# The first batch's plain-head results go straight into the mixing tiles, its token operands get buffers ahead of the last weights, and the tables load later

## The chip, the core and the metric

The kernel runs on one core of one Trainium2 chip. The metric is device time in microseconds (us) of that core, from the first to the last instruction and what lies around them. The engines are named as the profile names them: PE is TensorE (matmuls) and PEld its weight loads, DVE is VectorE, ACT is ScalarE, POOL is GpSimd, SP is SyncE, whose queue issues most DMAs. Each engine takes its instructions strictly in the order in which the program holds them.

## The reference

Eight batches of 576 tokens; eight heads of 64 columns, the first four with a plain window mask, the last four with a dilated one; then a mixing by Fourier transform over tokens and channels; then a normalised two-layer network with a residual.

```python
mask_plain = (rel >= 0) & (rel < 32)
mask_dil = (rel >= 0) & (rel < 128) & (rel % 4 == 0)
attn = softmax(where(mask[h], q @ k.T / 8, -1e9));  x = concat_heads(attn @ v)   # (8, 576, 512)
X = np.fft.fft(np.fft.fft(x, axis=1), axis=2)
u = x + np.real(X)
un = (u - mean(u)) / np.sqrt(var(u) + 1e-06)
out = u + np.maximum(un @ w_ch1, 0.0) @ w_ch2        # 512 -> 2048 -> 512
```

## The kernel before

All operations are put into one list (`Plan`), each with an engine, a planned cost and a priority; a planner written in the kernel goes through a model of time and emits the instructions in the order that it finds. The order on each engine is therefore fixed when the program is built. The numbers at the head of the file (`P_ST0`, `P_FD`, `P_MIX0`, `P_W` and so on) are due times, in units of one attention step, that set these priorities; `NSC2` and `NAV2` say for how many steps attention has two more PSUM banks.

**Attention** (`attention`, `attend_pair`, `attend`) makes 96 steps, 12 for each batch: two kinds of heads, two pairs of heads in each, three steps in each pair. A step is four score products on PE (L562), four masked row maxima on DVE (L571), four exponentials on ACT (L577), four transposes on PE (L590), a copy on ACT (L593), four products with the values on PE (L597), and three small operations on DVE (L605, L608, L609) that write the result tile `xt`. `store` (L644) sends `xt` to the DRAM tensors `xsp` and `xsm`, in which the token halves lie for the Fourier step.

**Mixing** (`mix`, one call for each batch) reads them back into four SBUF tiles `xs` and two tails `xtail` (L716, L725). `fold` adds and subtracts mirrored halves (L728, L730, L750, L752 on POOL, L742, L744 on DVE, L746, L747 on ACT); then come transforms along the tokens (L779, with tables `seq` and `tail`) and along the channels (L825, with tables `chn` and `alt`), the sums `u` (L693, L695 on POOL) and `normalise`. For the first batch `turned` transposes the normalised tokens on PE (L678) and splits them into a high and a low part (L685 on ACT, L686 on DVE) in a token tile `ut`; for the others the rows go through DRAM.

**Early network work** (`fill`): six of the 16 hidden blocks are computed for all 36 groups of 128 tokens, two in a call, while attention still runs: `up` (L959) needs a token tile `ut` and weights, `down` (L975) the hidden tile and weights. The rest of the network (L1228, L1283, L1316) follows once attention and mixing are done.

**Weights**: the twelve tiles for `fill` arrive as 64-bit floats. `prep_w` has each narrowed to 32 bits by four DVE operations (L900, L903, L906, L909) and one on ACT (L898), and split into a high part (L915 on ACT) and a low part (L917 on POOL). The staging tile of a weight and the token tile `ut` come from one ring of four buffers (`utb`), handed out in the order in which the program asks for them: the twelve weights first, then the two token tiles of the first batch. Buffer 13 of that sequence can be taken when the 9th weight has been read for the last time, by its L917.

**Filler**: L508 multiplies zeros. Wherever the planner has no other work for PE before the first `up`, it puts pairs of these products; from the first `up` on it puts none.

## Time and profile before

| what | value |
|---|---|
| median of 3 runs | 1077.82 us (1077.35 to 1078.23) |
| the profiled execution | 1077.06 us |
| its span, first to last instruction | 1075.3 us |
| PE busy, share of the span | 1062.8 us, 99% |
| filler among it (L508) | 240 products, 42.5 us, 1.4 to 116.4 us |
| DVE busy | 770.8 us, 72% |
| first `up` of the early network work | at 118.08 us |

The groups of instructions say where an engine's time goes, the windows say it by stage, and the timeline gives the order in time with the idle time in square brackets. Two records that follow each other on an engine can overlap, so that the sum of groups is larger than the engine's busy time, and PE counts as busy while it multiplies zeros.

### The profile page before, as it was taken

Reading aid. Unit: us, or ns where it says so; the run is one execution under the profiler, and the core shown is the slowest. Engines: PE = TensorE matmul, PEld = TensorE weight load, DVE = VectorE, ACT = ScalarE, POOL = GpSimd, SP = SyncE. Lnnn points to the kernel's source line nnn. Section 1 sums busy time; section 2 is a strip of 40 time slices with the busy share of each in tenths; the row PEclk is TensorE's granted clock in tenths of the full one; section 3 lists DMA queues with packets and bytes.
Section 4 is the critical chain, followed back from the end, with each engine's and each line's share of the span. In section 5 each row is a group of like instructions: output and inputs, shape, how many; then the busy total and the mean of one; then the engine's idle time right before and its main releaser. Section 6 shows DMA issues by size and latency. Waiting matters only on the chain.

```text
span 1075.3 us, 21155 instructions
## 1 busy us (share of the span) xinstructions
PE 1062.8 (99%) x7675; PEld 957.3 (89%) x7675; DVE 770.8 (72%) x2384; ACT 515.5 (48%) x1282; POOL 278.0 (26%) x328
## 2 busy tenths in 40 slices
PE   8999999999999999999999999999999999999998
PEld 7898988888888989998989898989999988989987
DVE  5989988878866765866675667677676767675845
ACT  6876755566464533444343443525252525252522
POOL 1247364554633355132321110101010101010200
PEclk9999999999999999999999999999999999999999
DMA  9987464746644341634363302322323232232211
GB/s 345 301 253 229 147 194 138 215 142 188 191 134 144 98 128 41 194 121 126 129 158 96 101 26 54 108 71 96 73 91 84 86 87 82 69 100 81 79 60 40
DMA packets 103801, 137.10 MB, mean 128 GB/s; under 512 B 9145, under 2 KB 61817, under 8 KB 103697
## 3 DMA queue, kind: packets, MB, share of 16 engines
q1 hardware_dynamic: 100128, 126.85, 39.4%
q0 software_dynamic: 3040, 8.09, 2.5%
q8 instruction: 60, 0.98, 0.4%
q10 hardware_dynamic: 528, 0.82, 0.2%
q14 instruction: 45, 0.36, 0.1%
HBM read 97.92 MB, written 37.80 MB: 126 GB/s over the span
## 4 chain that ended last, share of the span: by engine, by line
PE 93%; DVE 2%; DMA 2%; ACT 1%; issue 0%; POOL 0%; POOLq 0%; ACTq 0%; DVEq 0%
PE bank L1228 23%; PE bank L1316 20%; PE bank L959 14%; PE bank L975 13%; PE bank L597 5%; PE bank L562 5%; PE bank L825 3%; PE bank L779 3%; PE bank L590 3%; PE bank L508 3%; PE bank L1283 1%; DMA vt<-in_v_dram 1%; DVE pm L571 1%; DMA ut<-in_w_dram 1%; ACT pm L577 1%; PE bank L801 1%
## 5 line engine op out<-in xcount | busy, mean ns | idle before, releaser
L1228 PE MATMUL bank<-low,wb 128*128 128x512 f32 x1080 | 260.4, 393 | 0.0
L1228 PEld LDWEIGHTS bank<-low,wb 128*128 128x128 f32 x1080 | 198.5, 188 | 40.8
L959 PE MATMUL bank<-ut,low 128*128 128x256 f32 x1296 | 170.8, 285 | 0.1
L959 PEld LDWEIGHTS bank<-ut,low 128*128 128x128 f32 x1296 | 160.4, 189 | 3.2 <-DVE low L967 0.5
L975 PE MATMUL bank<-low 128*128 128x512 f32 x648 | 154.3, 392 | 0.0
L577 ACT ACTIVATE pm<-pm,mx 96x128 f32<-96x128 f32 x384 | 130.7, 395 | 39.5 <-DVE mx L571 37.7
L1003 POOL DMA_INDIRECT ut<-us,flip_sb x20 | 40.6, 2028 | 406.6 <-DVE ut L1060 249.8
L975 PEld LDWEIGHTS bank<-low 128*128 128x128 f32 x648 | 119.3, 188 | 23.1
L1234 ACT ACTIVATE xa<-bank 128x256 f32<-128x256 f32 x90 | 34.3, 382 | 179.9 <-PE bank L1228 179.9
L571 DVE CUSTOM_DVE_ANT_0 pm<-bank,mask_sb 96x128 f32<-96x128 f32 x384 | 93.3, 278 | 30.3 <-PE bank L562 27.6
L1255 DVE TENSOR_TENSOR y<-xa 128x384 f32<-128x384 f32 x45 | 25.1, 557 | 106.5 <-ACT xa L1234 106.2
L967 DVE SCALAR_TENSOR_TENSOR low<-bank,low 128x256 fp32r<-128x256 f32 x108 | 45.5, 422 | 62.0 <-ACT low L965 61.4
L597 PE MATMUL bank<-vt,ptsb 128*96 128x65 f32 x768 | 80.7, 247 | 2.5 <-DVE xt L609 1.5
L597 PEld LDWEIGHTS bank<-vt,ptsb 128*96 128x96 f32 x768 | 75.8, 164 | 6.9 <-ACT ptsb L593 1.6
L965 ACT ACTIVATE low<-bank 128x256 fp32r<-128x256 f32 x108 | 41.4, 384 | 79.4 <-PE bank L959 78.9
L1316 PEld LDWEIGHTS bank<-w2s,low 128*128 128x128 f32 x588 | 73.8, 190 | 2.4
L1049 DVE TENSOR_TENSOR ut<-ut,bank 128x512 f32<-128x512 f32 (+1 forms) x136 | 73.2, 547 | 2.6 <-PE bank L1228 0.5
L1082 DVE STREAM_TRANSPOSE ut<-ut 128x512 f32<-128x512 f32 (+1 forms) x76 | 71.6, 982 | 4.4 <-DMA ut<-us 4.2
L1316 PE MATMUL bank<-w2s,low 128*128 128x256 f32 x588 | 74.4, 282 | 0.0
L562 PE MATMUL bank<-kb,tq 64*96 64x128 f32 x768 | 63.0, 286 | 3.2 <-DVE mx L571 1.5
L593 ACT COPY ptsb<-bank 128x384 f32<-128x384 f32 x96 | 45.3, 472 | 35.8 <-PE bank L590 28.2
L1316 PEld LDWEIGHTS bank<-w2s,hm 128*128 128x128 f32 x483 | 59.8, 189 | 1.9
(147 smaller groups left out, 1817.3 us busy)
## 6 DMA issues: line engine op xcount, KB each, us to landing
vt<-in_v_dram SPq DMA_DIRECT2D x32, 390.0 KB
us<-uc SPq DMA_DIRECT2D x36, 257.0 KB
tq<-in_q_dram SPq DMA_DIRECT2D x32, 288.0 KB
part<-row SPq DMA_DIRECT2D x36, 256.0 KB
wst<-in_w_dram SPq DMA_DIRECT2D x18, 512.0 KB
ut<-us SPq DMA_DIRECT2D x36, 256.0 KB
ut<-part SPq DMA_DIRECT2D x36, 256.0 KB
kb<-in_k_dram SPq DMA_DIRECT2D x31, 288.0 KB
```

Of the source, the lines that this page charges most:

```text
L562: nc.tensor.matmul(sc()[e][:QB, KB * n:KB * n + KB], lhsT=tq()[ps, QB * t:QB * t + QB], rhs=kb()[ps, QB * t:QB * t + KB], start=True, stop ...
L571: nc.vector.tensor_tensor_reduce(pm()[:, i], sc()[i % 2][:QB, KB * (i // 2):KB * (i // 2) + KB], mask_sb()[:, masks[blocks[i // 2]]], -0.1 ...
L577: add("ACT", 0.295, lambda i=i: nc.scalar.activation(out=pm()[:, i], in_=pm()[:, i], func=AF.Exp, bias=mx()[:, i:i + 1], scale=-1.0), ((mx ...
L593: add("ACT", act(4 * QB) - 0.05, lambda: nc.scalar.copy(out=pt().rearrange("p i q -> p (i q)"), in_=ps()[:, :4 * QB]), (ps,), (pt,), prio)
L597: add("PE", 0.173, lambda i=i: nc.tensor.matmul(av()[:QB, 65 * i:65 * i + 65], lhsT=pt()[:, i], rhs=vt()[:, i % 2, blocks[i // 2]], start= ...
L959: nc.tensor.matmul(z()[:, :n_tok], lhsT=wf()[:, a, kk], rhs=ut()[:, p, kk], start=(kk == 0 and n == 0), stop=(kk == KT - 1 and n == 2),)
L967: add("DVE", dve(n_tok), lambda: nc.vector.scalar_tensor_tensor(h()[:, 1, :n_tok], z()[:, :n_tok], 0.0, h()[:, 0, :n_tok].bitcast(F32), op ...
L975: nc.tensor.matmul(acc(), lhsT=h()[:, a, P * s:P * s + P], rhs=wf()[:, p], start=(first and n == 0), stop=(last and n == 2),)
L1049: add("DVE", dve(C if at in (outer, inner) else TOK1), lambda: nc.vector.tensor_tensor(out=blocks(part())[:, at], in0=blocks(part())[:, at ...
L1082: nc.vector.transpose(out=o[back], in_=x[:, g])
L1228: nc.tensor.matmul(z(), lhsT=wb1[NF1 + 2 * p + f]()[:, a, kk], rhs=ut()[:, x, kk], start=(kk == 0 and n == 0), stop=(kk == KT - 1 and n == 2),
L1316: nc.tensor.matmul(acc()[block // 2][:, TOK1 * (block % 2):TOK1 * (block % 2) + TOK1], lhsT=hl()[:, a, i], rhs=w2s[p]()[:, j, x], start=(o ...
```

## The change

It does five things.

1. For the first batch attention takes the dilated heads before the plain ones. The plain results are no longer stored to DRAM: `place` copies them by ten SBUF-to-SBUF DMAs on SP's queue into the left 256 columns of `xs` and `xtail`, and `fold` then loads only the right 256 columns from DRAM. Two small zero fills (`row`) stand at the start.
2. The two token tiles of the first batch are asked for after nine weights instead of after twelve (`NU0`, `NU1`); `mix` uses them (`uts`).
3. The first batch's `fold` has its twelve POOL operations on DVE (`NFD = 1`; `NUD` and `NLW` are 0 and move nothing).
4. The tables are no longer loaded from the start on. A one-element POOL copy of an attention result goes ahead of them: `seq` and `tail` follow after step 4, `chn` and `alt` after step 10 (steps counted from 0).
5. Two small operations of `normalise` become `tensor_scalar`, and new due times stand at the head of the file.

```diff
-NSC2, NAV2 = 20, 29
+NSC2, NAV2 = 21, 32
+NU0, NU1 = 9, 9
+NFD, NUD, NLW = 1, 0, 0
-T_SEQ, T_CHN = 20.0, 27.0
+NSEQ, NCHN = 4, 10
...
+    def along(out, in_, key, nbytes):
+        add("POOL", 0.06, lambda: nc.gpsimd.dma_start(out=out(), in_=in_), (gone,), (key,), -50.0, nbytes)
+
+    def tables_after(num, xt):
+        if num == NSEQ:
+            add("POOL", 0.3, lambda: nc.gpsimd.tensor_copy(out=gone(), in_=xt()[0:1, 0, 0, 0:1]), (xt,), (gone,), -50.0)
...
-        for dil in range(2):
+        for n, dil in enumerate((0, 1) if b else (1, 0)):
...
+    def place(u, val, xt, prio):
+        tiles = (xs[0], xs[2], xtail[0]), (xs[1], xs[3], xtail[1])
+        for n, (e, row, side, lo, rows) in enumerate((
...
+            dma(lambda x=x, p0=p0, side=side, lo=lo, rows=rows: nc.sync.dma_start(
+                out=x()[p0:p0 + rows, 0:C // 2], in_=val()[lo:lo + rows, side]),
+                (xt,), ((x, ("plain", u, n)),), prio + P_ST0, rows * 1024)
...
+            cs = slice(0 if b else C // 2, C)
...
-            add("POOL", pool(NEH), lambda: nc.gpsimd.tensor_tensor(
+            either(b < NFD, NEH, lambda on: on.tensor_tensor(
                 out=t1()[at], in0=xp()[at, 0:NEH], in1=xm()[at, C:C // 2 - 1:-1], op=ALU.add), (xp, xm), (t1,), prio)
...
-                ut = utb()
+                ut = utb() if b else uts[m]
...
-    for f in range(NF1):
-        prep_w(f, wa1[f], wa2[f], utb, (), P_W + P_WF * f)
+    uts = {}
+    for n in range(2 * NF1 + 1):
+        for m, after in enumerate((NU0, NU1)):
+            if n == after:
+                uts[m] = utb()
+        if n < 2 * NF1:
+            f, eng = n // 2, "DVE" if n < NLW else "POOL"
+            if n % 2 == 0:
+                prep_up(f, wa1[f], utb(), (), P_W + P_WF * f, eng)
+            else:
+                prep(w2[P * f:P * f + P], False, wa2[f], utb(), (), P_W + P_WF * f, eng)
```

What the two programs hold ahead of the first `up`: PE has 240 filler products before and 206 after, 148 and 132 value products, 168 and 156 score products, 88 and 72 transposes by `ident_sb`, and the same number of everything else. DVE has, up to the second low part of the first token tile, 39 and 27 narrowing operations of 128x512, 161 and 149 row maxima, 36 and 32 each of L605, L608 and L609, and 12 more additions and subtractions of `fold`; little else differs. The last 3097 products on PE and the last 622 instructions on DVE are the same.

On PE at the first `up`, the kernel before; `blank` is the filler, `uc` the normalised tokens of the first batch, `ut,low` the token tile and the weights:

```order
L508 MATMUL bank_142<-blank 128x256 x8
L590 MATMUL bank_137<-ident_sb,pm 128x96 x4
L508 MATMUL bank_142<-blank 128x256 x14
L597 MATMUL bank_138<-vt,ptsb 96x65 x3
L678 MATMUL bank_140<-ident_sb,uc 128x128 x4
L597 MATMUL bank_138<-vt,ptsb 96x65
L678 MATMUL bank_139<-ident_sb,uc 128x128 x4
L959 MATMUL bank_141<-ut,low 128x256 x3
```

The same place in the changed kernel:

```order
L511 MATMUL bank_142<-blank 128x256 x6
L613 MATMUL bank_138<-vt,ptsb 96x65 x3
L711 MATMUL bank_140<-ident_sb,uc 128x128 x4
L613 MATMUL bank_138<-vt,ptsb 96x65
L711 MATMUL bank_139<-ident_sb,uc 128x128 x4
L606 MATMUL bank_137<-perm_sb,pm 128x96 x4
L993 MATMUL bank_141<-ut,low 128x256 x9
```

The 22 filler products in these rows have become 6, and the first `up` comes after 33 attention steps instead of 37. (Line numbers of the changed kernel are 3 to 36 higher: L993 is the `up` of L959.)

On DVE just before and at the low part of the first token tile (`ut<-bank`), the kernel before; `ut<-ut` is the narrowing of a weight:

```order
L909 SCALAR_TENSOR_TENSOR ut<-ut 128x512
L903 SCALAR_TENSOR_TENSOR ut<-ut 128x512
L605 TENSOR_SCALAR sums<-bank_138 96x4
L571 ISA pm,mx<-bank_135,mask_sb 96x128
L571 ISA mx 96x1
L608 RECIPROCAL rinv<-sums 96x4
L906 SCALAR_TENSOR_TENSOR ut<-ut 128x512
L609 TENSOR_TENSOR xt<-bank_138,rinv 96x4x64
L686 TENSOR_TENSOR ut<-bank_140,ut 128x4x128
L686 TENSOR_TENSOR ut<-bank_139,ut 128x4x128
```

The same place in the changed kernel:

```order
L587 ISA mx 96x1
L587 ISA pm,mx<-bank_135,mask_sb 96x128
L587 ISA mx 96x1
L587 ISA pm,mx<-bank_136,mask_sb 96x128
L587 ISA mx 96x1
L944 SCALAR_TENSOR_TENSOR ut<-ut 128x512
L587 ISA pm,mx<-bank_135,mask_sb 96x128
L587 ISA mx 96x1
L625 TENSOR_TENSOR xt<-bank_141,rinv 96x4x64
L719 TENSOR_TENSOR ut<-bank_140,ut 128x4x128
L719 TENSOR_TENSOR ut<-bank_139,ut 128x4x128
```

The low part stood among the narrowing of the 10th weight; it now stands after that of the 6th and in the middle of the 7th.

On SP at the first batch's mixing tiles, the kernel before; `x` and `xt` on the left are the tiles `xs` and `xtail`:

```order
L716 DMA x_161<-xsp_59 128x512
L716 DMA x_162<-xsm_67 128x512
L716 DMA x_163<-xsp_59 128x512
L716 DMA x_164<-xsm_67 128x512
L725 DMA xt_165<-xsp_59 32x512
L725 DMA xt_166<-xsm_67 32x512
L725 DMA xt_165<-xsm_67 1x512
L725 DMA xt_166<-xsm_67 1x512
```

The same place in the changed kernel, from the last of eight loads of the right halves on; here the `xt` on the right is an attention result:

```order
L763 DMA xt_167<-xsm_67 1x256
L642 DMA x_162<-xt 96x256
L642 DMA x_162<-xt 32x256
L642 DMA x_164<-xt 64x256 x2
L642 DMA xt_166<-xt 32x256
L642 DMA x_165<-xt 63x256
L642 DMA xt_167<-xt 32x256
L642 DMA xt_166<-xt 1x16x16
L642 DMA x_163<-xt 31x256
L642 DMA x_165<-xt 65x256
L642 DMA x_163<-xt 96x256
```

The loads of whole rows have become loads of half rows, and ten copies follow, the last of them into the tile that the first fold reads.

## Rows read from the trace of the kernel before

**Rows 1.** The page's head and its part 1: busy us, share, instructions.

```profile
span 1075.3 us, 21155 instructions
...
PE 1062.8 (99%) x7675; PEld 957.3 (89%) x7675; DVE 770.8 (72%) x2384; ACT 515.5 (48%) x1282; POOL 278.0 (26%) x328
```

**Rows 2.** Windows: length, busy us of each engine, PE clock, DMA share, GB/s.

```profile
0.00:25.00 25.00, 21.37 (x200) 19.20 (x201) 14.33 (x105) 14.90 (x43) 3.60 (x10) 1.00 1.01 342
...
100.00:118.00 18.00, 17.82 (x171) 16.70 (x172) 16.82 (x77) 11.40 (x32) 6.43 (x8) 1.00 0.80 251
...
118.00:135.00 17.00, 17.00 (x153) 15.36 (x153) 15.22 (x63) 12.71 (x36) 7.55 (x9) 1.00 0.36 114
...
400.00:1000.00 600.00, 599.74 (x3770) 541.25 (x3770) 407.23 (x759) 243.73 (x540) 92.63 (x81) 1.00 0.33 94
```

**Rows 3.** Groups on PE, 0 to 118 us: xcount | busy, mean ns | idle before.

```profile
L508 PE MATMUL bank<-blank 128*128 128x256 f32 x240 | 42.5, 313 | 1.4 <-DVE kb L502 1.4
...
L597 PE MATMUL bank<-vt,ptsb 128*96 128x65 f32 x296 | 30.8, 247 | 0.7 <-ACT ptsb L593 0.7
...
L562 PE MATMUL bank<-kb,tq 64*96 64x128 f32 x336 | 28.3, 287 | 1.8 <-DMA tq<-in_q_dram 1.5 <-DVE mx L571 0.3
...
L590 PE MATMUL bank<-ident_sb,pm 96*128 96x96 f32 x88 | 11.9, 250 | 0.0
```

**Rows 4.** Timeline of PE: start, us, instruction, [idle before it and its releaser].

```profile
9.77 1.44 PE L508 MATMUL bank<-blank 128*128 128x256 f32 x10
11.05 0.81 PE L597 MATMUL bank<-vt,ptsb 128*96 128x65 f32 x8
...
13.67 1.12 PE L562 MATMUL bank<-kb,tq 64*96 64x128 f32 x16 [1.47 <-DMA tq<-in_q_dram]
...
118.08 0.60 PE L959 MATMUL bank<-ut,low 128*128 128x256 f32 x3
```

**Rows 5.** Timelines of ACT, POOL and DVE at the first token tile.

```profile
113.04 0.62 ACT L915 CAST low<-ut 128x512 fp32r<-128x512 f32 x1 [1.30 <-DVE ut L909]
...
113.73 1.29 POOL L917 TENSOR_TENSOR low<-ut,low 128x512 fp32r<-128x512 f32 x1 [7.17 <-DMA tq<-in_q_dram]
...
115.05 1.08 ACT L685 CAST ut<-bank 128x512 fp32r<-128x512 f32 x2 [0.54 <-POOL low L917]
...
115.83 1.27 DVE L686 TENSOR_TENSOR ut<-bank,ut 128x512 fp32r<-128x512 f32 x2
```

**Rows 6.** Groups on DVE by form, 0 to 118 us.

```profile
L571 DVE CUSTOM_DVE_ANT_0 pm<-bank,mask_sb 96x128 f32<-96x128 f32 x162 | 39.1, 278 | 12.3 <-PE bank L562 10.1 <-ACT ut L898 1.0 <-PE bank L590 0.5
...
L609 DVE TENSOR_TENSOR xt<-bank,rinv 96x256 f32<-96x256 f32 x36 | 14.7, 413 | 0.1
...
L906 DVE SCALAR_TENSOR_TENSOR ut<-ut 128x512 uint32<-128x512 uint32 x10 | 9.2, 923 | 0.1
...
L903 DVE SCALAR_TENSOR_TENSOR ut<-ut 128x512 uint32<-128x512 uint32 x10 | 7.1, 707 | 0.0
...
L909 DVE SCALAR_TENSOR_TENSOR ut<-ut 128x512 f32<-128x512 f32 x10 | 6.9, 691 | 0.0
...
L608 DVE RECIPROCAL rinv<-sums 96x4 f32<-96x4 f32 x36 | 5.9, 166 | 0.1
...
L605 DVE TENSOR_SCALAR sums<-bank 96x4 f32<-96x4 f32 x37 | 5.4, 149 | 4.3 <-PE bank L597 4.0
...
L900 DVE TENSOR_SCALAR ut<-ut 128x512 uint32<-128x512 uint32 x10 | 4.6, 477 | 0.6 <-DMA ut<-in_w_dram 0.6
...
L742 DVE TENSOR_TENSOR ee<-t,t 128x257 f32<-128x257 f32 x3 | 1.3, 419 | 0.0
```

**Rows 7.** DMA queues, 0 to 45 us: the one that POOL fills with tables.

```profile
q0 software_dynamic: 1440, 2.82, 19.8%
```

**Rows 8.** Timeline of POOL at the first fold.

```profile
59.02 0.73 POOL L728 TENSOR_TENSOR t<-x,x 128x257 f32<-128x257 f32 x1
```

**Rows 9.** Waits on POOL over the whole span: us in total, times, longest.

```profile
POOL t L728 <- DMA x<-xsm: 16.1, 5, 6.9
```

More of the change, by code (lines that the diff above doesn't have):

```diff
@@ L478, in fused_kernel @@
     half = fixed(keep, [P, 1], F32, "half")
+    gone = fixed(heads, [1, 1], F32, "gone")
     kbs = [fixed(heads, [P, WIN + S], F32, f"kb{i}") for i in range(NKB)]
@@ L511, in start @@
             zero(t, "DVE", 0.07, lambda t=t: nc.vector.memset(t()[:, C:C + 1], 0.0), "pad")
+        for t, p in ((xs[1], 0), (xtail[1], 32)):
+            zero(t, "DVE", 0.1, lambda t=t, p=p: nc.vector.memset(t()[p:p + 1, 0:C // 2], 0.0), "row")
         def gaps():
@@ L521, in start @@
             ), (blank,), ((xsm[b], "zero"),), 12 * b + 6, 2048)
-        for i in range(2):
-            for m in range(2):
-                add("POOL", 0.06, lambda i=i, m=m: nc.gpsimd.dma_start(out=seq_sb[i]()[:, m], in_=seq[i, m]),
-                    (), ((seq_sb[i], m),), 6 + i, P * 2 * NSP * 4, at=T_SEQ + i)
-                add("POOL", 0.06, lambda i=i, m=m: nc.gpsimd.dma_start(out=chn_sb[i]()[:, m], in_=chn[i, m]),
-                    (), ((chn_sb[i], m),), 9 + i, P * 2 * NEP * 4, at=T_CHN + i)
@@ L528, in start @@
-        add("POOL", 0.06, lambda: nc.gpsimd.dma_start(out=tail_sb(), in_=tail), (), (tail_sb,), 6.5, P * 3 * NSP * 4, at=T_SEQ + 0.5)
-        add("POOL", 0.06, lambda: nc.gpsimd.dma_start(out=alt_sb(), in_=alt), (), (alt_sb,), 8, P * NEP * 4, at=T_SEQ + 4)
+    def along(out, in_, key, nbytes):
[3 more added lines that the diff above has]
+            add("POOL", 0.3, lambda: nc.gpsimd.tensor_copy(out=gone(), in_=xt()[0:1, 0, 0, 0:1]), (xt,), (gone,), -50.0)
+            for i in range(2):
+                for m in range(2):
+                    along(lambda i=i, m=m: seq_sb[i]()[:, m], seq[i, m], (seq_sb[i], m), P * 2 * NSP * 4)
+                if i == 0:
+                    along(tail_sb, tail, tail_sb, P * 3 * NSP * 4)
+        if num == NCHN:
+            add("POOL", 0.3, lambda: nc.gpsimd.tensor_copy(out=gone(), in_=xt()[0:1, 0, 0, 0:1]), (xt,), (gone,), -50.0)
+            for i in range(2):
+                for m in range(2):
+                    along(lambda i=i, m=m: chn_sb[i]()[:, m], chn[i, m], (chn_sb[i], m), P * 2 * NEP * 4)
+                if i == 0:
+                    along(alt_sb, alt, alt_sb, P * NEP * 4)
@@ L533, in attention, with attend_pair @@
     def attention(b, when):
-        for dil in range(2):
+        for n, dil in enumerate((0, 1) if b else (1, 0)):
             xts = [attw("xt", [QB, 2, 4, D], F32, 3) for _ in range(3)]
             for j in range(2):
-                attend_pair(b, dil, j, xts, lambda u: when(6 * dil + 3 * j + u))
-    def attend_pair(b, dil, j, xts, when):
+                attend_pair(b, dil, j, 2 * n + j, xts, lambda u: when(6 * n + 3 * j + u))
+    def attend_pair(b, dil, j, at, xts, when):
         lead = when(0) + (P_QK if b else P_QK0)
-        first = b == 0 and dil == 0 and j == 0
+        first = b == 0 and at == 0
@@ L626, in store @@
         plus, minus = xsp[b], xsm[b]
+        if not dil and not b:
+            place(u, val, xt, prio)
+            return
         if not dil:
@@ L665, in normalise @@
             out=r0(), in0=ve(), in1=half(), op=ALU.pow), (ve, half), (r0,), prio + 1)
-        add("DVE", 0.13, lambda: nc.vector.scalar_tensor_tensor(
+        add("DVE", 0.07, lambda: nc.vector.tensor_scalar(
             r1(), ve(), r0(), r0(), op0=ALU.mult, op1=ALU.mult), (ve, r0), (r1,), prio + 1)
@@ L690, in fused_kernel, with either, add_u @@
     rest = {}
-    def add_u(dst, src, near, far, bufs_r, buf_w, prio):
-        add("POOL", pool(NEH), lambda: nc.gpsimd.tensor_tensor(
+    def either(dve_, n, go, r, w, prio):
+        on = nc.vector if dve_ else nc.gpsimd
+        add("DVE" if dve_ else "POOL", (dve if dve_ else pool)(n), lambda: go(on), r, w, prio)
+    def add_u(b, dst, src, near, far, bufs_r, buf_w, prio):
+        either(b < NUD, NEH, lambda on: on.tensor_tensor(
             out=dst()[:, 0:NEH], in0=src()[:, 0:NEH], in1=near()[:, 0:NEH], op=ALU.add), bufs_r, buf_w, prio)
-        add("POOL", pool(C - NEH), lambda: nc.gpsimd.tensor_tensor(
+        either(b < NUD, C - NEH, lambda on: on.tensor_tensor(
             out=dst()[:, NEH:C], in0=src()[:, NEH:C], in1=far()[:, 255:0:-1], op=ALU.add), bufs_r, buf_w, prio)
```

58 lines of the change are left out of this document (29 added, 29 removed), and 3 rows, old and new, of the table tiles.

## The prediction

> **What bounds the kernel now.** I read the page's head first, then the windows, then the groups on PE, then the timeline around the first `up`. PE is busy in 99% of the span and DVE in 72% [rows 1], so PE looks like the bound from end to end. The windows show two regimes. From 400 to 1000 us PE is busy for 599.74 of 600 us with real products [rows 2], and the last 3097 products stand in the same order in both programs: nothing is to be had there. In the first 118 us 240 of PE's products are filler, 42.5 us of busy time [rows 3], and they end where the first `up` begins, at 118.08 us [rows 4]. There DVE is the bound: 16.82 of the last 18 us, when PE's 17.82 are largely zeros [rows 2]. So the time of the kernel is PE's useful work, which does not change, plus what PE spends without useful work. The change can only move the second part, and nearly all of that lies ahead of 118 us.
>
> What releases the first `up` is in the timelines: ACT's high part of the 9th weight at 113.04, POOL's low part at 113.73 to 115.02, then the token tile's high parts on ACT at 115.05, its low parts on DVE at 115.83, and the `up` at 118.08 [rows 4, 5]. The token tile takes the buffer that the 9th weight leaves; POOL's 7.17 us of idle time ahead of that low part [rows 5] show that the chain waited for DVE's narrowing, not for POOL.
>
> **The balance.** If the first `up` starts at time t in the changed kernel, with useful work worth d less done ahead of it, the gain is 118.1 - t - d, as long as PE then finds work as it does now. Both numbers come from counts of instructions and from rows.
>
> **What is missing ahead of it on PE (d).** 16 value products, 12 score products and 16 transposes, four steps' worth but for four scores. By the groups a value product is 2 x 30.8/296 = 0.21 us (two records each), a score product 2 x 28.3/336 = 0.17, a transpose 11.9/88 = 0.135 [rows 3]: 3.3 + 2.0 + 2.2 = 7.5 us. These busy times overlap their neighbours: a filler product is 42.5/240 = 0.177 us by its group [rows 3], but ten of them run from 9.77 to 11.05, 0.128 each [rows 4]. With the same ratio d would be 5.4. I take 6.5, the middle.
>
> **When PE's own queue would be there.** 34 filler products less at 0.128 are 4.4 us (6.0 by the group's 0.177), d is 6.5, and the wait of 1.47 us for `tq` at 13.67 [rows 4] goes, if the loads come sooner (below): 118.1 - 12.4 = 105.7. If nothing held PE, the gain would be 5.9 us.
>
> **When DVE's queue would be there.** Ahead of the first token tile's low parts DVE loses 12 narrowing operations (39 to 27), because that tile now takes the buffer of the 6th weight instead of the 9th, 12 row maxima, and four each of the three small operations of a step; it gains the 12 operations of the first fold. By the groups a narrowing is (9.2 + 7.1 + 6.9 + 4.6)/40 = 0.70 us, a maximum 39.1/162 = 0.24, the small three 14.7/36 + 5.9/36 + 5.4/37 = 0.72, and a fold operation of 128x257 1.3/3 = 0.43 [rows 6]. So -8.3 - 2.9 - 2.9 + 5.2 = -8.9 us. Here too records overlap (a maximum is 278 ns long and adds 241, [rows 6]); with that ratio it is -7.7. I take -8, and since DVE is busy in 16.82 of 18 us there [rows 2], -8.6 of the clock. The two `tensor_scalar` edits shorten operations of one column, four normalisations ahead of the place; at well under 1 us they stay inside these bounds.
>
> Three things shift this. **Tables:** 2.82 MB of them move in the first 45 us [rows 7], most of it issued before 5 us, while the DMA share is 1.01 and 342 GB/s move [rows 2]. Loading them after steps 4 and 10 takes them from in front of the q, k and v tiles. The visible price is the 1.47 us wait for `tq` [rows 4], which DVE shares; the most is the whole 2.82/0.342 = 8.2 us, the least nothing, since the tables then meet the weights. I take -1.5, the row of the wait. The Trainium skill (DMA: Bandwidth & Descriptors, section Issuing engines are not separate DMA queues) states that DMAs of any engine run on the same 16 DMA engines and interleave; the DMA share of 1.01 agrees. By that rule alone the nearer value would be the 8.2, and what binds then is PE's own queue at 105.7.
>
> **The copies into the mixing tiles:** the fold now waits for ten copies on SP, the last of them into the tile that it reads first; behind that wait stand all of DVE's next steps, and PE behind DVE. The first fold began at 59.02 on POOL before [rows 8]. Folds have waited for their loads 16.1 us in five waits, 6.9 at the longest [rows 9]: 0 to 6.9. In DVE's order four steps, 4 x (4 x 0.24 + 0.72) = 6.7 us, lie between the last plain result and the fold, and they hide most of ten short copies. I take +0.5, near the lower end. The skill's same page (Rules for kernel authors) says that transfers under 64 KB pay mostly overhead and should be joined into larger ones, which speaks against ten copies of 1 to 96 KB; its section on the anatomy of a DMA gives about 2.0 us as the fixed part. With that as the wait the gain would be 1.5 us smaller. No run here prices such a copy yet. **POOL:** the fold's move takes 12 operations off its queue; nobody waits for POOL before the first `up` but the weight's low part, so this is nothing.
>
> So t = 118.1 - 8.6 - 1.5 + 0.5 = 108.5, later than PE's own 105.7: DVE still decides. The gain is 118.1 - 108.5 - 6.5 = 3.1 us.
>
> **Behind the first `up`** the weights that were passed have to be made, and the last of them gets its buffer only when the first call's `up` products are done. From 118 to 135 us PE is busy 17.00 of 17, DVE 15.22 [rows 2]: DVE has a tenth to spare. Between 0 and 4 us could come back there; I take 0 for the forecast, because the steps moved behind bring PE work of their own (6.5 us) along with DVE's, and the rest is the first rival. Everything later is PE with a backlog, and free.
>
> The profiled execution took 1077.06 us, 0.76 less than the median of 1077.82. 1077.06 - 3.1 = 1073.96; on the median's scale 1074.7, which I predict (-0.29%).
>
> **The rivals.** *Given back behind the first `up`.* There is no filler any more, PE has one batch's calls and attention, and DVE carries up to 12 narrowings (8.3 us) more; with a tenth of some 42 us to spare (4.4 us), up to 3.9 us of PE waiting replace the filler. For it: DVE's 15.22 of 17 [rows 2]. Against it: four steps of PE work moved along. The result is a gain between -0.8 and 1.1: about 1077.5. *The first token tile waits on POOL.* The 6th weight's low part now stands on POOL behind the second batch's first fold, whose loads stand on SP behind the first batch's normalised rows. If that fold waits as the longest one did, 6.9 us [rows 9], t is 115.4 and the gain 118.1 - 115.4 - 6.5 = -3.8: 1081.6, slower. It decides from t = 111.6 on, where the gain is gone. Against it: such a wait came once in the span, and DVE needs its time as well. *DVE is quicker than its sum.* If the loads come earlier by more than the one wait, PE's own queue binds at 105.7 and the gain is 5.9: 1071.9. For it: the DMA share of 1.01 in the first 25 us [rows 2].
>
> **How the numbers follow.** Forecast 0.44, given back 0.24, slower by POOL's chain 0.17, quicker 0.15. About 0.2% (2.2 us) is what a measurement of this kernel can tell from no change. Faster: the quicker case and nine tenths of the forecast, 0.55. Same: nearly all of "given back" and the forecast's small end, 0.28. Slower: 0.17. The range takes in the quicker case and reaches up to the nearer half of the slower one: 1071.3 to 1079.8.
>
> **What the profile would show.** The first `up` at 108 to 109 us with 206 filler products ahead of it; the wait for `tq` near 13 us gone; the first fold on DVE without a wait over 1 us; PE's idle time from there to 150 us under 2 us. A first `up` after 111.6 us, or PE waits of 2 to 4 us right behind it, would make the prediction wrong; a different busy time of PE after 600 us would refute the frame.

## The result: 1067.24 us, and the profile after

The changed kernel takes 1067.24 us (median of 4, 1066.83 to 1067.98) beside 1077.68 us of the kernel before on the same chip: a ratio of 0.9904, interval 0.9892 to 0.9916, or 10.4 us less. The forecast was 3.1 us less, with a range down to 1071.3. The direction was right; the size was not, and the time lies below the range. The page's head, part 1 (busy us, share, instructions), to be held against [rows 1]:

```profile
span 1065.7 us, 21052 instructions
...
PE 1057.6 (99%) x7641; PEld 952.4 (89%) x7641; DVE 775.7 (73%) x2398; ACT 516.1 (48%) x1282; POOL 272.4 (26%) x318
```

The windows, with the places of [rows 2] moved along with the first `up` (length; busy us of PE, PEld, DVE, ACT, POOL; PE clock; DMA share; GB/s):

```profile
0.00:25.00 25.00, 23.55 (x224) 21.35 (x225) 16.72 (x119) 17.28 (x50) 3.21 (x10) 1.00 0.98 344
...
87.00:105.00 18.00, 17.86 (x181) 15.83 (x180) 16.87 (x105) 16.02 (x48) 6.46 (x8) 1.00 0.77 256
...
105.00:122.00 17.00, 16.95 (x166) 15.95 (x165) 15.22 (x61) 13.00 (x35) 8.43 (x8) 1.00 0.54 164
...
400.00:1000.00 600.00, 599.08 (x3755) 539.89 (x3754) 420.84 (x790) 246.64 (x545) 105.68 (x89) 1.00 0.33 95
```

PE's groups from 0 to 105 us (xcount | busy, mean ns | idle before), as in [rows 3], and PE's timeline at the places of [rows 4]:

```profile
L511 PE MATMUL bank<-blank 128*128 128x256 f32 x206 | 35.5, 313 | 1.4 <-DVE kb L505 1.4
...
L613 PE MATMUL bank<-vt,ptsb 128*96 128x65 f32 x264 | 27.2, 248 | 0.5 <-DVE xt L625 0.4
...
L578 PE MATMUL bank<-kb,tq 64*96 64x128 f32 x312 | 25.6, 287 | 0.0
```

```profile
10.07 1.43 PE L511 MATMUL bank<-blank 128*128 128x256 f32 x10
...
12.41 1.12 PE L578 MATMUL bank<-kb,tq 64*96 64x128 f32 x16
...
104.78 1.31 PE L993 MATMUL bank<-ut,low 128*128 128x256 f32 x9
```

The filler is down from 240 products to 206. The wait for `tq` is gone: the 16 score products of L578 follow at 12.41 with nothing in brackets, where [rows 4] has 1.47 us. The first `up` (L993) starts at 104.78 us instead of 118.08, 13.3 us earlier; 9.6 were forecast. The first token tile on POOL, ACT and DVE, as in [rows 5]; the weight's low part waited 2.48 us for ACT's high part, and nothing on PE waited for it:

```profile
99.47 1.27 POOL L955 TENSOR_TENSOR low<-ut,low 128x512 fp32r<-128x512 f32 x1 [2.48 <-ACT low L953]
...
100.85 1.05 ACT L718 CAST ut<-bank 128x512 fp32r<-128x512 f32 x2
...
102.53 1.27 DVE L719 TENSOR_TENSOR ut<-bank,ut 128x512 fp32r<-128x512 f32 x2
```

Behind the first `up`, 232 us of each kernel (118 to 350 us before, 105 to 337 us after):

```profile
118.00:350.00 232.00, 228.29 (x1944) 204.03 (x1943) 181.82 (x852) 134.63 (x376) 111.77 (x155) 1.00 0.55 165
```

```profile
105.00:337.00 232.00, 231.51 (x1951) 207.71 (x1951) 183.04 (x821) 136.48 (x375) 102.69 (x139) 1.00 0.59 176
```

PE's idle time there fell from 3.71 to 0.49 us. From 600 us on both are busy without a gap (400.00 of 400 us).

**Where the 10.4 us come from.** The starts of all PE products give a balance in the prediction's own terms. Each useful product is priced by the median distance to the next start for its kind in the trace before (a product of two records as one); the change of that sum is d, and what remains up to the first `up` is filler and everything else.

| up to the first `up`, us | before | after | difference |
|---|---|---|---|
| first `up` starts | 118.08 | 104.78 | 13.30 |
| useful products ahead of it (d) | 68.52 | 63.13 | 5.39 |
| filler, start to start | 36.92 | 31.04 | 5.88 |
| PE's other time (waits, and starts further apart than the medians) | 12.64 | 10.60 | 2.04 |

So 13.30 - 5.39 = 7.9 us are gained at the first `up`, and that is the last two rows: less filler, and less waiting. By the end of the span the gain has grown to 9.85 us. (The two profiled spans differ by 9.6, the medians by 10.4.) Less filler is bookkeeping, not a cause: the planner lays filler where it expects PE to wait. The experiments ask what those waits were.

### The profile page after: what moved, and what is told of

Read it like the earlier page. It is cut to its first block, busy times and chain, and to the rows that moved or that the text cites. A ratio compares the mean times of both kernels' runs of the same rounds, so it can differ in the third digit from the quotient of the medians.

```text
span 1065.7 us, 21052 instructions
## 1 busy us (share of the span) xinstructions
PE 1057.6 (99%) x7641; PEld 952.4 (89%) x7641; DVE 775.7 (73%) x2398; ACT 516.1 (48%) x1282; POOL 272.4 (26%) x318
## 4 chain that ended last, share of the span: by engine, by line
PE 96%; DMA 2%; DVE 1%; ACT 1%; issue 0%; SPq 0%; DVEq 0%
PE bank L1271 23%; PE bank L1359 20%; PE bank L993 14%; PE bank L1009 13%; PE bank L613 6%; PE bank L578 5%; PE bank L863 3%; PE bank L817 3%; PE bank L606 3%; PE bank L511 2%; PE bank L1326 1%; DMA xsm<-xt 1%; PE bank L839 1%; DMA wst<-in_w_dram 1%; ACT pm L593 0%; DMA us<-uc 0%
## 5 line engine op out<-in xcount | busy, mean ns | idle before, releaser
L993 PE MATMUL bank<-ut,low 128*128 128x256 f32 x1296 | 171.3, 285 | 0.9 <-DVE low L1001 0.9
L993 PEld LDWEIGHTS bank<-ut,low 128*128 128x128 f32 x1296 | 160.5, 189 | 3.8 <-DVE low L1001 1.4
L593 ACT ACTIVATE pm<-pm,mx 96x128 f32<-96x128 f32 x384 | 128.2, 393 | 40.1 <-DVE mx L587 36.5
L1277 ACT ACTIVATE xa<-bank 128x256 f32<-128x256 f32 x90 | 34.4, 382 | 180.3 <-PE bank L1271 180.3
L1298 DVE TENSOR_TENSOR y<-xa 128x384 f32<-128x384 f32 x45 | 25.1, 557 | 107.0 <-ACT xa L1277 106.7
L578 PE MATMUL bank<-kb,tq 64*96 64x128 f32 x768 | 63.0, 286 | 0.1
L1359 PE MATMUL bank<-w2s,hm 128*128 128x256 f32 x483 | 60.2, 280 | 0.0
```

Source lines behind the costliest of these rows:

```text
L578: nc.tensor.matmul(sc()[e][:QB, KB * n:KB * n + KB], lhsT=tq()[ps, QB * t:QB * t + QB], rhs=kb()[ps, QB * t:QB * t + KB], start=True, stop ...
L593: add("ACT", 0.295, lambda i=i: nc.scalar.activation(out=pm()[:, i], in_=pm()[:, i], func=AF.Exp, bias=mx()[:, i:i + 1], scale=-1.0), ((mx ...
L993: nc.tensor.matmul(z()[:, :n_tok], lhsT=wf()[:, a, kk], rhs=ut()[:, p, kk], start=(kk == 0 and n == 0), stop=(kk == KT - 1 and n == 2),)
L1359: nc.tensor.matmul(acc()[block // 2][:, TOK1 * (block % 2):TOK1 * (block % 2) + TOK1], lhsT=hl()[:, a, i], rhs=w2s[p]()[:, j, x], start=(o ...
```

## The experiments

In the first four groups the order is frozen: every engine keeps its instructions in the order of the kernel it was made from, but for the edit. In the last group the planner makes a new order. "Gain there" is 118.1 - t - d as above, "end" how much earlier the last product of the profiled span starts than in the kernel before, and the difference is what is won or lost behind the first `up`. The medians beside it are of the timed runs, with the ratio to the kernel before.

**Late tables.** The tables go back to the start in the changed kernel (a_tables_early), and behind steps 4 and 10 in the kernel before (b_tables_late).

```diff
-        for o in order:
-            o.fn()
+        for o in order:            # the tables' loads first
+            if o.num in self.early:
+                o.fn()
+        for o in order:
+            if o.num not in self.early:
+                o.fn()
```

> The changed kernel with its order kept on every engine, but the tables seq, tail and alt are loaded from the start on, as in the kernel before (the chn table stays late). Theory 1 (the gain comes from DVE's shorter queue ahead of the first up): the wait for tq near 13 us comes back, +1.5 us on 1067.2, so 1068 to 1069. Rival (the early loads account for most of what the sum missed): DVE's idle time ahead of the first up grows back by 3.7 us, 1070.5 to 1071.5.

> The kernel before with its tables loaded behind steps 4 and 10, order of everything else unchanged. Theory 1 (the loads' place is worth what it was in the changed kernel, where early tables cost 1.9 us and brought a wait of 1.42 us for tq back): 1075.5 to 1076.7, the wait for tq at 12 us gone. Rival (in this order the loads are not late, or the tables now collide with the weights): 1077.2 or more.

The first took 1069.14 us (0.9920, 0.9907 to 0.9933), 1.9 more than the changed kernel; gain there 6.5 instead of 7.9. The second took 1076.78 us (0.9990, 0.9981 to 1.0000): the first `up` comes 1.2 us earlier, as expected; the profiled execution has lost that by its end, the timed ones keep it. PE's timeline with early tables:

```profile
12.06 0.50 PE L613 MATMUL bank<-perm_sb,pm 96*128 96x96 f32 x4
...
13.81 1.12 PE L585 MATMUL bank<-kb,tq 64*96 64x128 f32 x16 [1.25 <-DMA tq<-in_q_dram]
```

The wait for `tq` is back at the place of [rows 4], 1.25 us long (an expectation above says 1.42), and the first `up` comes 1.4 us later (106.17). So the term of the tables (-1.5 at the first `up`) was right, place and size. The Trainium skill's rule (DMA: Bandwidth & Descriptors, section Issuing engines are not separate DMA queues) is that DMAs of all engines run on the same 16 and interleave; the trace agrees with its direction. The 8.2 us that the prediction set beside that rule, as if each byte of the tables stood in front, are far from the 1.4 measured.

**Copies and fold, order frozen.** In a_round_trip the copies into mixing's tiles become four stores to DRAM and eight loads of the left halves; in a_fold_pool the 12 operations of the first fold stand on GpSimd. (There are eleven copies, as the rows of the changed kernel's order show, x2 counted twice; the texts ahead of this say ten.)

```diff
-                out=x()[p0:p0 + rows, 0:C // 2], in_=val()[lo:lo + rows, side]),
+                # to plus/minus in DRAM; after the last store, the left halves of the tiles
...
-        on = nc.vector if dve_ else nc.gpsimd
+        on = nc.gpsimd
```

> The changed kernel with its order kept on all engines but SP, where the ten copies of the first batch's plain results are replaced at their place by stores to DRAM and eight loads of the left halves. Theory 1 (the copies are hidden by the four attention steps ahead of the fold): the fold, next in DVE's order, now waits for a store and a load one after the other, some 3 to 5 us, of which the first up sees all: 1069 to 1072. Rival (the direct copies change nothing, because the fold's place in the order is late enough): 1067.0 to 1067.8.

> The changed kernel with its order kept, but the twelve additions and subtractions of the first batch's fold run on POOL again, at the same place of the program. Theory 1: DVE's queue ahead of the first up is 4.2 us shorter but waits for POOL, whose operations of this kind took 0.73 us each in the trace of before; since DVE has other work only behind them in order, 0 to +4 us: 1067 to 1071. Rival (POOL's low parts and the fold compete for the same place, so the move to DVE is what freed the weights): more than +4 us.

1067.01 us (0.9905, 0.9891 to 0.9920) and 1069.04 us (0.9922, 0.9909 to 0.9935). In this order the copies bring nothing by themselves, the fold on DVE at most 1.8 us; the second run's profiled execution (1067.18) shows none of it at the end. The Trainium skill's rule against transfers below 64 KB (same page, Rules for kernel authors) finds no price here: eleven copies of 1 to 96 KB and the longer way with larger loads take the same time. The 2.0 us that the prediction puts beside them stand in that page's section for DMAs that GpSimd issues; these copies are issued on SP's queue, and no run prices a single one. In a_fold_pool 4.2 us of fold operations less on DVE did not bring the first `up` forward (105.4), but DVE also waited 2.6 us for GpSimd's fold there, so this run does not show by itself whether DVE's length sets it.

**Narrowing.** The prediction's frame was that DVE decides. In b_narrow_short 15 narrowing operations of the kernel before work on one column instead of 512.

```diff
+        part[0] += 1
+        k = 1 if 6 <= part[0] <= 10 else C
...
-            bits(F32), mag(), F64_MIN, bits(F32), op0=ALU.is_ge, op1=ALU.mult), (m,), (v,), prio)
+            bits(F32)[:, 0:k], mag()[:, 0:k], F64_MIN, bits(F32)[:, 0:k], op0=ALU.is_ge, op1=ALU.mult), (m,), (v,), prio)
```

> The kernel before, in which 15 narrowing operations of the 6th to 10th part of the weights treat one column instead of 512 (those parts of the weights are not computed; 14 of the 15 stand ahead of the first token tile's low parts, some 8 us of DVE). Order and filler (240 products) unchanged. Theory 1 (the filler has been cut to DVE's length, so both queues end nearly together and PE's own queue is next): the first up at most 2 us earlier, 1075.5 to 1077.5. Rival (DVE alone holds the first up): 4 to 8 us earlier, 1069 to 1073.

1077.60 us (0.9996, 0.9986 to 1.0005). The window before the first `up` and its start, to be held against [rows 2] and [rows 4]:

```profile
100.00:118.00 18.00, 17.66 (x170) 16.35 (x170) 13.45 (x79) 11.52 (x32) 6.22 (x8) 1.00 0.86 259
...
118.59 0.60 PE L965 MATMUL bank<-ut,low 128*128 128x256 f32 x3
```

DVE is busy 13.45 of 18 us instead of 16.82, and PE is not a moment earlier: 17.66 busy, first `up` at 118.59. The view that says why is the chain of waits of the kernel before (the work that ended last, followed back at each step to what released it), from 100 to 118 us, shares of the chain by line:

```profile
by line: PE bank L508 47.6%; PE bank L562 19.1%; PE bank L597 18.3%; PE bank L590 10.1%; PE bank L678 4.4%; DVE pm L571 1.1%; issue 0.2%; DVE mx L571 0.1%
```

PE's own lines hold 99.5% of it, the filler alone (L508) 47.6%. At that place DVE was busy, but PE was the one that came last. In the changed kernel, from 87 to 105 us, PE comes last too; its lines hold 94%:

```profile
by line: PE bank L578 28.7%; PE bank L613 21.4%; PE bank L511 21.0%; PE bank L606 14.8%; PE bank L711 7.0%; ACT pm L593 2.2%; ACT ptsb L609 2.1%; DVE pm L587 1.6%; issue 1.2%; PE bank L993 0.8%; DVE mx L587 0.1%; DVEq L587 0.0%
```

This holds for orders with their filler in place: where the filler stands was laid down by the planner, and no run makes a new order with shorter narrowing.

**Filler.** If PE's own queue decides, leaving filler out should pay, unless the filler covers a wait. Left out were: the last 84 of 240 products before (b_late_out), the last 54 of 206 after (a_late_out), every second one of those 54 (a_half_late), every second of all 206 (a_half_filler), every fourth of all (a_three_quarters); and with the short narrowing the 84 (b_narrow_late) or half of them (b_narrow_half).

```diff
-                for _ in range(2):
+                turns[0] += 1
+                for _ in range(2 if turns[0] <= 76 else 0):
                     nc.tensor.matmul(spin()[:, :2 * P], lhsT=blank()[:, :P], rhs=blank()[:, P:3 * P], start=True, stop=True)
```

> The kernel before without its last 84 filler products (those behind about 90 us, 11.6 us from start to start); its order is otherwise unchanged, and no result depends on them. Theory 1 (the prediction's frame: ahead of the first up DVE is the bound, and these products only fill PE's waits): the first up stays within 1 us of 118.1, the time at 1077 to 1078.5. Rival (PE's own queue holds the first up, and the filler is a price of its own): the first up comes 5 to 11 us earlier, 1066 to 1073. In between, both queues end nearly together: 1 to 4 us earlier, 1074 to 1077.

> The changed kernel without its last 54 filler products (those behind about 80 us, 7.8 us from start to start), order otherwise unchanged. Theory 1 (DVE's queue also holds the first up here): the first up within 1 us of 104.8, time 1066 to 1068. Rival (with DVE's queue shortened PE's own queue has become the bound, as the prediction's case 'DVE is quicker than its sum' has it): the first up 4 to 8 us earlier, 1059 to 1063.

> The changed kernel with one of every two filler products behind about 80 us left out, 27 of 54, some 3.9 us. Theory 1 (PE's own queue holds the first up here too): 1063.5 to 1065.5, faster than both kernels, if the granted clock stays at 1.00. Rival (waits for DVE or ACT take the place of the filler): 1066.5 to 1068; with the clock lost as without all late filler: 1068 to 1071.

> The changed kernel with its order kept, but every filler operation of the plan emits one product of zeros instead of two: 103 instead of 206, without any effect on what is computed. Theory 1 (DVE's chain decides when the first up starts, and the filler only fills waits): first up within 1 us of 104.8 and 1066 to 1068. Rival (PE's own queue decides): 103 products at 0.12 to 0.13 us, 12 to 13 us faster, 1054 to 1056. A third outcome, slower than 1068.5, would mean that the clock granted to PE falls when the zeros are missing.

> The changed kernel with every fourth filler product left out (155 of 206 stay), order otherwise unchanged. Theory 1 (part of the filler is a price of PE's own queue): 1063 to 1066 if the clock holds at 1.00, faster than both kernels. Rival (waits for the chains through DVE, ACT and GpSimd take its place): 1066.5 to 1068.5; a lost clock adds up to 5.

> The same 15 narrowing operations on one column, and besides the last 84 filler products left out as in the run without late filler, which took 1080.71 us. Theory 1 (DVE holds the first up, the filler only covers its waits): now the time that DVE lost is gained, first up 5 to 9 us earlier than the 120.2 of that run, 1069 to 1075, with less of a fall of the granted clock. Rival (something else, a load or PE's own products, holds the first up when the filler is gone): within 2 us of 1080.7.

> The kernel before with the 15 narrowing operations on one column (those parts of the weights are not computed; alone 1077.60 us, first up at 118.6) and with one of every two filler products behind about 90 us left out, 42 of 84, some 5.8 us. Theory 1 (PE's own queue, filler included, holds the first up, and DVE no longer needs the time): first up 4 to 6 us earlier, 1071.5 to 1074 if the granted clock stays at 1.00 between 90 and 125 us. Rival (the chain of score, maximum, exponential, transpose and value through PE, DVE and ACT holds it, whatever DVE has to do): within 1.5 us of 1077.6.

| run | left out, of | us, median | ratio, interval | first `up` | filler, us | other, us |
|---|---|---|---|---|---|---|
| b_late_out | 84 of 240 | 1080.71 | 1.0025, 1.0015 to 1.0036 | 120.2 | 25.6 | 26.1 |
| b_narrow_late | 84 of 240 | 1079.34 | 1.0020, 1.0008 to 1.0032 | 119.2 | 25.3 | 25.4 |
| b_narrow_half | 42 of 240 | 1077.99 | 1.0000, 0.9988 to 1.0012 | 119.2 | 34.4 | 16.2 |
| a_late_out | 54 of 206 | 1071.29 | 0.9926, 0.9903 to 0.9949 | 107.9 | 23.1 | 21.7 |
| a_half_late | 27 of 206 | 1067.99 | 0.9912, 0.9895 to 0.9929 | 104.2 | 29.0 | 12.1 |
| a_half_filler | 103 of 206 | 1066.63 | 0.9887, 0.9870 to 0.9903 | 106.8 | 25.9 | 17.7 |
| a_three_quarters | 51 of 206 | 1068.55 | 0.9908, 0.9891 to 0.9925 | 106.7 | 26.8 | 16.8 |

No order became faster than the kernel it was made from by more than the spread. b_late_out and a_late_out came out slower than either of their theories had it; a_half_late, a_half_filler, b_narrow_late and, at the median, b_narrow_half lie where waits take the place of the filler, a_three_quarters at the edge of that. In the table, too, the filler's column falls and the last one rises. Two things make it so, and one run shows the second without the first. One is the clock; windows of b_late_out:

```profile
95.00:100.00 5.00, 3.96 (x33) 3.05 (x33) 4.54 (x32) 2.84 (x8) 4.20 (x7) 1.00 0.87 276
...
100.00:105.00 5.00, 3.91 (x32) 2.87 (x32) 4.65 (x20) 3.32 (x10) 2.24 (x3) 0.81 0.94 291
...
105.00:110.00 5.00, 3.38 (x21) 2.92 (x23) 3.64 (x30) 3.21 (x10) 1.24 (x2) 0.50 0.98 340
```

PE was busy 3.96 of 5 us at full clock (2.4 GHz); in the next 5 us, 3.91 busy, the granted clock fell, and from 105 to 120 us it stood at 0.50, the lower of its two levels (1.2 GHz). With all filler PE was busy 17.82 of 18 us there, at 1.00 [rows 2].

The other is a second chain, nearly as late as PE's queue. a_half_late shows it, for in its profiled execution the clock stayed at 1.00 up to the first `up` and far beyond. Its window ahead of the first `up`, two pieces of its chain of waits near the end, and what PE waited for there:

```profile
80.00:104.20 24.20, 22.50 (x223) 18.91 (x223) 21.95 (x138) 19.60 (x58) 9.31 (x13) 1.00 0.86 267
...
102.03 0.61 DVE ut L721
102.68 0.75 PE bank L713 x4
...
PE bank L713 <- DVE ut L721: 0.4, 1, 0.4
```

With 27 filler products left out the first `up` comes 0.6 us earlier (104.2), not by the 3.9 us that PE's queue alone would give. From 87 us on the chain now lies on DVE by 57% and on ACT by 26%, and PE waits for DVE's low part of the token tile. So in the changed kernel DVE's chain ends within 0.6 us of PE's queue. In b_narrow_half, with DVE's work and half the late filler of the kernel before gone, the chain of waits at 96 to 105 us (clock still 1.00) does not run through PE either; line numbers are 2 higher here than in the kernel before:

```profile
97.59 1.36 POOL x L697 x2
...
100.33 2.34 issue
102.70 1.01 POOL r L666
...
103.73 0.75 DVE r L668
```

It is the way from mixing through GpSimd's sums (L697) and power function (L666) to the normalised rows, which the first token tile needs; for 2.34 us of it the view names no wait. So theory 1 and its rival were both half right: where the clock held, b_narrow_half took 1074.36 and 1074.62 us in single executions (granted clock 1.000 and 0.999), 3.0 to 3.2 us below b_narrow_short, of the 5.8 us left out; in the others (0.993 to 0.996) 1077 to 1079.6. PE's queue, mixing's chain and DVE end within a few us of one another. None of the runs without filler beats the changed kernel at the median. a_half_filler's executions run from 1062.40 us (clock 1.000) to 1068.87 (0.992): the one in which the clock held was 4.8 us faster than the changed kernel, so part of its early filler may be a price, but that execution has no profile.

**New orders.** Which part of the change allows the shorter order? Here the planner knows the edit. The due times stay as they were set for the whole change, so a part's price below is that of taking it out without setting new times.

```diff
-NU0, NU1 = 9, 9
+NU0, NU1 = 12, 12                       # a_buf12: the buffers' old place
...
-NFD, NUD, NLW = 1, 0, 0
+NFD, NUD, NLW = 0, 0, 0                 # a_fold_planned: the fold on GpSimd
...
-        if not dil and not b:            # a_dram_planned: no copies
-            place(u, val, xt, prio)
-            return
```

a_old_times puts the old numbers of the due times into the changed kernel, b_new_times the new ones into the kernel before; b_buf9n is the kernel before with the new numbers and the buffers behind the 9th part.

> The changed kernel with the token operands' buffers taken behind the 12th part of the weights again instead of behind the 9th; the order is planned anew, so 39 narrowing operations stand ahead of the first token tile's low parts instead of 27, and 292 filler products instead of 206. Early loads, late tables, copies, fold on DVE and the new due times stay. Theory 1 (the gain is the 12 narrowing operations that no longer stand ahead): the first up at 116 us or later, time 1075 to 1080. Rival (the gain comes from the loads' order and the due times, the buffers' place is secondary): 1067 to 1072.

> The changed kernel planned with the due times of the kernel before: structure, buffers, loads and copies of the change, the old numbers that set the order (196 filler products, 26 narrowing operations ahead of the first token tile's low parts). Theory 1 (structure carries the gain): 1066 to 1070. Rival (the new due times carry half of it or more, mostly behind the first up): 1072 to 1078.

> The kernel before planned with the due times of the change, nothing else changed (272 filler products, 71.2 us of useful products ahead of the first up instead of 68.5). Theory 1 (structure and numbers belong together, neither brings the gain alone): 1078 to 1090, first up later than 118. Rival (the numbers alone carry a good part of the gain): 1068 to 1075.

> The kernel before with two things of the change only: the token operands' buffers taken behind the 9th part of the weights, and the new due times; early tables, the way over DRAM, the fold on GpSimd and the old small operations stay; planned anew (210 filler products, 33 narrowing operations ahead of the first token tile's low parts). Theory 1 (the buffers' place with matching due times carries the gain, the rest some 2 us): 1067 to 1071. Rival (the copies, the fold on DVE and the late tables are what lets the tile come early): 1074 to 1080.

> The changed kernel with the first batch's plain results going over DRAM as before (no copies into the mixing tiles), due times unchanged, planned anew: 222 filler products, 60.5 us of useful products ahead of the first up instead of 63.1. Theory 1 (the copies allow an order that the way over DRAM does not, which the frozen order hid): 1070 to 1075. Rival (they bring nothing in a new order either): 1066 to 1068.5.

> The changed kernel with the first fold planned on GpSimd again (198 filler products, 59.7 us of useful products ahead of the first up). Theory 1 (GpSimd's slower fold pushes the mixing back, or its weights): 1070 to 1075. Rival (the fold's engine does not matter, as in the frozen order, where it cost 0 to 1.8 us): 1066 to 1069.

| run | us, median | ratio, interval | first `up` | d | gain there | end | behind |
|---|---|---|---|---|---|---|---|
| changed kernel | 1067.24 | 0.9904, 0.9892 to 0.9916 | 104.8 | 5.4 | 7.9 | 9.9 | +1.9 |
| a_buf12 | 1079.64 | 1.0016, 0.9999 to 1.0033 | 126.2 | -3.4 | -4.8 | -2.5 | +2.3 |
| b_new_times | 1081.32 | 1.0030, 1.0018 to 1.0041 | 125.9 | -2.7 | -5.1 | -3.9 | +1.3 |
| b_buf9n | 1074.22 | 0.9959, 0.9945 to 0.9974 | 104.7 | 7.9 | 5.5 | 2.9 | -2.7 |
| a_dram_planned | 1072.23 | 0.9945, 0.9928 to 0.9961 | 103.7 | 8.0 | 6.4 | 4.3 | -2.0 |
| a_fold_planned | 1075.40 | 0.9980, 0.9968 to 0.9992 | 99.4 | 8.8 | 9.9 | 2.8 | -7.1 |
| a_old_times | 1097.62 | 1.0181, 1.0164 to 1.0198 | 102.4 | 8.7 | 6.9 | -19.5 | -26.5 |

a_buf12, a_dram_planned and b_new_times came out as their theory 1 had it, b_buf9n at its rival's lower end; a_fold_planned is 0.4 us slower than its theory 1 allowed, and a_old_times far slower than either of its theories. The first `up` goes by the buffers' place: 99.4 to 104.8 us wherever the token operands come behind the 9th part of the weights, whatever the due times and the rest; 126 with the new numbers and 118 with the old ones where they come behind the 12th. With all else of the change in place, that is 12.4 us of time (a_buf12). How much of it is kept is decided behind the first `up`, and there the parts matter. With the fold on GpSimd PE finds less:

```profile
99.40 0.84 PE L993 MATMUL bank<-ut,low 128*128 128x256 f32 x5
...
100.00:337.00 237.00, 234.47 (x1979) 207.40 (x1978) 187.61 (x855) 142.12 (x397) 105.32 (x143) 1.00 0.59 174
```

2.53 us of 237 idle, where the changed kernel has 0.49 of 232, and 3.4 us less useful work stands ahead. But idle time is not most of what is lost behind. From the first `up` to 600 us PE is idle for 4.2 us in the kernel before, 1.4 in the changed one, 4.5 in a_fold_planned, 1.9 in a_dram_planned and 3.6 in b_buf9n: for these three the "behind" of -7.1, -2.0 and -2.7 is not in waits of PE that the trace shows, and where it lies stays open. With the old due times it is worst, and there PE does wait, 15.3 us idle up to 600 us; two windows of a_old_times, and PE's two largest waits from 105 to 165 us (total, times, longest):

```profile
135.00:145.00 10.00, 7.67 (x49) 5.79 (x47) 9.29 (x41) 4.99 (x14) 6.85 (x10) 0.68 0.68 196
...
145.00:155.00 10.00, 7.98 (x42) 6.34 (x43) 8.37 (x46) 5.33 (x16) 6.28 (x9) 0.50 0.64 183
...
PE bank L613 <- DVE xt L625: 2.2, 3, 0.9
...
PE bank L578 <- DVE mx L587: 1.2, 1, 1.2
```

PE has no filler left there and little beside attention; it waits for DVE's results, is busy 7.67 and 7.98 of 10 us, and the clock falls to 0.68 and 0.50 on top (to 1.00 again from 165 us on). So structure and numbers belong together: the old structure with the new numbers +3.5 us, the new one with the old numbers +19.5, both new -10.4.

## Why the prediction fell short

**Right.** The frame: nothing changes behind 600 us; the gain is 118.1 - t - d plus what happens behind. The signs of PE's and DVE's counts and of the tables. The 12 narrowing operations came to 8.30 us (start to start, 24.87 to 16.57), as costed. The tables' 1.5 came to 1.4. POOL's chain did not hold the tile, which was the slower rival. PE's idle time from the first `up` to 152 us was 0.45 of 47 us. The copies' 0.5 was nothing: the fold's operations stand on DVE from 50.66 us on without a wait.

**The step that failed: "So t = 118.1 - 8.6 - 1.5 + 0.5 = 108.5, later than PE's own 105.7: DVE still decides."** Two counts of queues were set against each other, and the later one was believed. It was mis-sized, and it was not the one that came last.

The size: the count for DVE moved the tile by 9.6 us, and it moved by 13.3. DVE's work up to the tile fell by 9.6 us (97.3 to 87.7, start to start), not by 8: the groups' sum of 8.9 had been taken down to 8 for overlap, the fold's 12 operations cost 4.2 us and not 5.2, and the normalisations saved another 1, while maxima and small operations gave 1.5 less than costed. DVE's idle time fell by 3.7 us (19.8 to 16.1), not by 1.6. The DVE groups after, as in [rows 6]:

```profile
L587 DVE CUSTOM_DVE_ANT_0 pm<-bank,mask_sb 96x128 f32<-96x128 f32 x152 | 36.1, 279 | 8.5 <-PE bank L578 7.6 <-PE bank L606 0.3
...
L944 DVE SCALAR_TENSOR_TENSOR ut<-ut 128x512 uint32<-128x512 uint32 x7 | 5.9, 837 | 0.0
...
L766 DVE TENSOR_TENSOR t<-x,x 128x257 f32<-128x257 f32 x2 | 0.8, 422 | 0.0
```

What came last: PE's queue. In the kernel before, b_narrow_short took 8 us off DVE for nothing, and the chain of waits lies on PE by 99.5%; in the changed kernel by 94%. DVE's 16.82 of 18 us [rows 2] showed an engine that was busy, not the one that was waited for. Still DVE is close: a_half_late meets its chain 0.6 us earlier than PE's queue ends. A right count of DVE's queue would thus have given nearly the measured t.

The count for PE, 105.7 forecast and 104.78 measured, is in part luck. Its 12.4 us were 4.4 of filler, 6.5 of useful work and 1.5 of waiting; measured were 5.9, 5.4 and 2.0.

**A second term that was mis-sized: d.** Taken as 6.5, it was 5.39. The timeline had shown which of the two prices holds: ten filler products from 9.77 to 11.05 [rows 4] take 0.128 us each, not the 0.177 of their group. With 5.4 the forecast's gain would have been 4.2 us and not 3.1. The rival "quicker" would not have moved: where PE's own queue binds, d brings t forward and is then subtracted from the gain, so that it cancels; its 5.9 us are filler and waiting alone (7.9 measured). The filler went the other way than d: its 34 products came to 5.9 us, 0.17 each.

**The bound that had one side: behind the first `up`.** "Between 0 and 4 us could come back there" left no room below nothing, and 1.9 us were gained there. PE's idle time up to 600 us fell from 4.2 to 1.4 us; most of that is waits of the old order for DVE's maxima and results, 2.6 us from 118 to 350 us, where the new order has 0.3. The rival "given back" did not come in the changed kernel. Four of the orders above do lose behind the first `up`, 2.0 to 26.5 us; that PE waits for DVE, as the rival has it, makes PE's idle time there much longer than before in a_old_times alone (15.3 against 4.2 us). The new due times had no term of their own in the sum: with the changed structure, the old numbers lose 26.5 us behind the first `up`.

Together: t 3.7, d 1.1, behind 1.9, and 3.1 forecast make 9.8 us, the 9.85 of the balance. What stays open is why the whole change gains behind the first `up` where the orders without the copies, the fold or the new numbers lose: the runs price each part's absence under one set of numbers, and the prices (12.4 for the buffers, 8.2 for the fold, 5.0 for the copies, 1.9 for the tables) do not add up to 10.4. They are not shares. Nor do they say why the buffers' place lets the planner start the first `up` earlier: in a_buf12 the 12 narrowing operations move with the buffers.

## What to carry to other kernels

Where idle time is filled with dummy work, read who comes last from the chain of waits, not from who is busy, and ask how far behind it the next chain ends; and price work that is moved by distances between starts, not by the lengths of records. An edit in a frozen order tells what a part costs in place, which may be nothing, because the filler stays; what a part allows shows only when the order is made anew, and then the numbers that set the order are part of the change. A bound on what follows behind needs both signs.

## What the runs showed of the hardware

The filler keeps PE's clock as well as its queue. In a_half_filler, with 103 filler products over the first 107 us, PE was busy 3.86 of 5 us from 20 us on, still at 1.00; in the next 5 us the granted clock was 0.53, and from 30 to 35 us PE ran at the lower level, busy 5.00 of 5 us with fewer products (32 instead of 41); from 40 us on it was at 1.00 again:

```profile
20.00:25.00 5.00, 3.86 (x41) 3.08 (x39) 5.00 (x32) 3.33 (x11) 0.00 (x0) 1.00 1.12 394
25.00:30.00 5.00, 4.54 (x26) 3.73 (x27) 1.30 (x9) 3.47 (x11) 1.26 (x1) 0.53 0.72 228
30.00:35.00 5.00, 5.00 (x32) 4.19 (x31) 3.64 (x25) 3.33 (x12) 0.00 (x0) 0.50 0.94 284
...
40.00:45.00 5.00, 5.00 (x58) 4.25 (x56) 4.52 (x31) 4.36 (x13) 3.49 (x6) 1.00 0.32 54
```

In the timeline of b_late_out the longest wait of PE from 92 us until the clock fell at 103 us was this one:

```profile
102.13 0.89 PE L599 MATMUL bank<-vt,ptsb 128*96 128x65 f32 x8 [0.69 <-DVE xt L611]
```

a_half_filler's executions spread by 6.5 us with the granted clock of the span (1.000 to 0.992), where the changed kernel's spread by 1.15. And an operation of one column per partition is no small matter on DVE: the `scalar_tensor_tensor` of L666 in the kernel before took 328 ns in the mean of 36, the `tensor_scalar` that replaced it (L699) 265, while a `tensor_scalar` with constants (L701) takes 146. The mean hides the spread: L666 has a median of 218 ns and single ones up to 792, L699 a median of 266 and none above 276. So the new form is steadier, and not shorter in the typical case; what made the long ones long is not shown.
